# First 320 tokens of q and k by two other rings in float32, two pairs' scores in other banks, and the end by column halves

## The chip, the cores and the metric

The kernel runs on one core of one Trainium2 chip. The metric is device microseconds per execution, the median of several runs. Before: 324.33 us (three runs, 324.32 to 324.61). Executions of the kernel before fall into a fast state and a slow one, some 2% longer; only fast runs are compared. Ratios below are the mean time of one kernel's fast runs over the mean time of the other's fast runs of the same rounds, so they are not quite the ratio of the medians that stand beside them. The experiments ran on several chips, each beside runs of the kernel before on the same chip.

## The reference, cut to what matters

```python
B, H, S, D = 8, 8, 576, 64                      # batch, heads, tokens, head dim; all float32
scores = q @ k^T / sqrt(D), only |i - j| <= 32 kept
x = (softmax(scores) @ v)  -> (4608 tokens, 512)
h = x @ w_in                                    # 512 x 2048
g = where(h > 0, h, exp(min(h, 0)) - 1)
out = g @ w_out                                 # 2048 x 512
```

A banded attention feeds a feed-forward network (FFN). The FFN's matmuls are most of TensorE's work; the attention of the first pairs of query blocks has to be done before the FFN can start, while weights and later batches still load.

## The kernel before

Batch 0's q and k come by GpSimd's DMA queue, cast to bf16 on the way. Two heads share the 128 partitions (head `a` of a pair on partitions 64a to 64a+63, nine tokens in each partition):

```python
def load_qk(b, nm, half):
    src = {"q": q, "k": k}[nm]
    src = src[b, half * HP:(half + 1) * HP]          # four heads, all 576 tokens
    ...
    src = src.rearrange("(n a) (p t) d -> (a p) n (t d)", a=2, t=TPW)   # TPW = 9
    nc.gpsimd.dma_start(out=t, in_=src)
```

Scores, softmax, the transposed inputs of the FFN, and the end:

```python
def QK(i):
    psS = psS_p.tile([128, 2, 2, HP, QB], FP32, name="psS", tag="psS")   # one buffer
    ...
def SM(i):
    nc.scalar.activation(pu, live.pop(("S", i)), AX.Exp, scale=SCALE)
...
NPX = 8            # x of pairs 0 to 7 transposed by TensorE, of all later ones by DMA
...
def YC(t, c):      # last block: two copies of half the columns each, one after the other
    nc.scalar.copy(y[:, 0:DM // 2], ys[t, c][:, 0:DM // 2])
    nc.vector.tensor_copy(y[:, DM // 2:DM], ys.pop((t, c))[:, DM // 2:DM])
```

The instructions are ordered by a plan, a list of operations with ranks and dependences; `RING` is the order of GpSimd's loads (q, k, v and the quarters of w_in and w_out).

The softmax here doesn't subtract the row's maximum and nothing guards it: scores larger than these inputs give would overflow.

Of the kernel before, what the change touches and what calls it, by code (L numbers as in the profile page):

```python
# [156 lines left out]
def kernel(  # L157
# [20 lines left out]
    PR = 96  # L178
    TPP = S // PR
    TPW = S // QB  # L180
    NWB = 3
# [7 lines left out]
    const = ctx.enter_context(tc.tile_pool(name="const", bufs=1))  # L189
    bfp = ctx.enter_context(tc.tile_pool(name="bfp", bufs=4))  # L190
# [29 lines left out]

    def make_masks():
        mf = ep.tile([128, 4, QB], FP32, name="mf", tag="e")
        nc.gpsimd.memset(mf, 1.0)
        for mi in range(3):
            m = mf[:, mi, :]
            nc.gpsimd.affine_select(
                out=m, in_=m, compare_op=ALU.is_ge, fill=0.0,
                base=0, pattern=[[-1, QB]], channel_multiplier=1)
            nc.gpsimd.affine_select(
                out=m, in_=m, compare_op=ALU.is_ge, fill=0.0,  # L230
                base=2 * WIN, pattern=[[1, QB]], channel_multiplier=-1)
        for lo, key in ((0, QB), (QB, 0)):
            m = mf[lo:lo + QB, 3, :]
            nc.gpsimd.affine_select(
                out=m, in_=m, compare_op=ALU.is_ge, fill=0.0,
                base=key, pattern=[[-1, QB]], channel_multiplier=1)
            nc.gpsimd.affine_select(
                out=m, in_=m, compare_op=ALU.is_ge, fill=0.0,
                base=2 * WIN - key, pattern=[[1, QB]], channel_multiplier=-1)
        nc.gpsimd.affine_select(  # L240
            out=mf[:, 1, :], in_=mf[:, 1, :], compare_op=ALU.is_ge,
            fill=0.0, base=-WIN, pattern=[[0, QB]], channel_multiplier=1)
        nc.gpsimd.affine_select(
            out=mf[:, 2, :], in_=mf[:, 2, :], compare_op=ALU.is_ge,
            fill=0.0, base=(128 - WIN) - 1, pattern=[[0, QB]],
            channel_multiplier=-1)
        nc.gpsimd.tensor_copy(masks, mf)


    def wide(b):  # L250
        return b < NWB

    def load_qk(b, nm, half):
        src = {"q": q, "k": k}[nm]
        src = src[b, half * HP:(half + 1) * HP]
        if half == 0:
            live[nm, b] = bfp.tile(
                [128, HP, TPW * D] if wide(b) else [PR, H, TPP * D], BF16,
                name="bf", tag="bf")
        t = live[nm, b]  # L260
        if wide(b):
            t = t[:, half * HP // 2:(half + 1) * HP // 2]
            src = src.rearrange("(n a) (p t) d -> (a p) n (t d)", a=2, t=TPW)
        else:
            t = t[:, half * HP:(half + 1) * HP]
            src = src.rearrange("h (p t) d -> p h (t d)", t=TPP)
        nc.gpsimd.dma_start(out=t, in_=src)  # L267

    def T(b, nm, hp):
        src = live[nm, b]  # L270
        n = 2 * hp + (nm == "k")
        pool, tag = (psH_p, "psH") if b == 0 and n % 4 else (psT_p, "psT")
        pt = pool.tile([128, TPW, QB] if wide(b) else [128, TPP, PR], BF16,
                       name=tag, tag=tag)
        live["T", b, nm, hp] = pt
        if wide(b):
            for j in range(TPW):
                for a in (0, QB):
                    nc.tensor.transpose(pt[a:a + QB, j, :],  # L279
                                        src[a:a + QB, hp, j * D:(j + 1) * D],  # L280
                                        ident[a:a + QB, a:a + QB])
            return
        for j in range(TPP):
            nc.tensor.transpose(pt[:, j, :],
                                src[:, 2 * hp:2 * hp + 2, j * D:(j + 1) * D],
                                ident[0:PR, 0:PR])

    def E(b, nm, hp):
        pt = live.pop(("T", b, nm, hp))
        if nm == "k":  # L290
            dst = kT[b % NKB][:, hp, WIN:WIN + S]
        else:
            dst = qT[b % NKB][:, hp, :]
        dst = dst.rearrange("c (p t) -> c p t", t=TPW if wide(b) else TPP)
        src = pt.rearrange("c t p -> c p t")
        if EVAC[b, nm, hp] == "ACT":
            nc.scalar.copy(dst, src)  # L297
        else:
            nc.vector.tensor_copy(dst, src)  # L299
# [59 lines left out]
    def QK(i):  # L359
        psS = psS_p.tile([128, 2, 2, HP, QB], FP32, name="psS", tag="psS")  # L360
        for s in range(2):
            b, qb = divmod(2 * i + s, NQB)
            for h in range(H):
# [7 lines left out]
                for p0, p1, c in parts:  # L371
                    nc.tensor.matmul(  # L372
                        psS[p0:p1, h % 2, s, hp, :],
# [4 lines left out]
    def SM(i):  # L378
        pu = pup.tile([128, 2, 2, HP, QB], BF16, name="pu", tag="pu")
        nc.scalar.activation(pu, live.pop(("S", i)), AX.Exp, scale=SCALE)  # L380
# [32 lines left out]
    def RN(i, g):  # L413
        o = live.pop(("O", i, g))
        if g == 0:
            live["X", i] = xsp.tile([128, H, D], BF16, name="xs", tag="xs")
# [6 lines left out]
    def X(i):  # L423
# [6 lines left out]
        if i >= NPX:  # L430
# [52 lines left out]
    def ypool(t, c):  # L483
        if t < NT - 1:
            return psY_p, "psY"
        return ((psY_p, "psY"), (psO_p, "psO"), (psT_p, "psT"),
                (psS_p, "psS"))[c % 4]

    def Y(t, c, part):
        if part == 0:  # L490
            pool, nm = ypool(t, c)
            ys[t, c] = pool.tile([128, DM], FP32, name=nm, tag=nm)
        ps = ys[t, c]
        for fo in range(YQ * part, YQ * part + YQ):
            nc.tensor.matmul(ps, lhsT=gs[t][:, fo, c * 128:(c + 1) * 128],  # L495
                             rhs=w_out_sb[:, fo, :],
                             start=(fo == 0), stop=(fo == NFO - 1))

    def YC(t, c):
        y = yp.tile([128, DM], FP32, name="y", tag="y")  # L500
        if (t, c) == yseq[-1]:
            nc.scalar.copy(y[:, 0:DM // 2], ys[t, c][:, 0:DM // 2])
            nc.vector.tensor_copy(y[:, DM // 2:DM], ys.pop((t, c))[:, DM // 2:DM])
        else:
            nc.scalar.copy(y, ys.pop((t, c)))  # L505
        ys[t, c] = y

    def OUT(t, c):
        r = (tiles[t][0] + c) * 128
        y = ys.pop((t, c))  # L510
        if (t, c) == yseq[-1]:
            nc.sync.dma_start(out[r:r + 128, 0:DM // 2], y[:, 0:DM // 2])
            nc.scalar.dma_start(out[r:r + 128, DM // 2:DM], y[:, DM // 2:DM])
        else:
            nc.sync.dma_start(out[r:r + 128, :], y)
# [13 lines left out]
    NPX = 8  # L529

    P = Plan({"SP": 0.8, "ACT": 0.8, "POOL": 0.8, "DVE": 6.0})
# [20 lines left out]
    def prank(i):  # L552
# [3 lines left out]
    NV3 = 4  # L556
    LQ0, LQD = 64.0, 2.4
# [5 lines left out]
    RING = [  # L563
        ('L', 0, 'q', 0),
# [3 lines left out]
        ('ID',),  # L568
        ('LV', 0, 0),
        ('LV', 0, 2),  # L570
        ('MS',),
# [3 lines left out]
        ('WI', 1),  # L575
        ('L', 1, 'q', 0),
        ('L', 1, 'k', 0),
        ('WI', 2),
        ('LV', 0, 8),
        ('WI', 3),  # L580
        ('L', 1, 'q', 1),
        ('L', 1, 'k', 1),
        ('WO', 0),
        ('LV', 1, 0),
        ('WO', 1),
        ('LV', 1, 2),
        ('WO', 2),
        ('LV', 1, 4),
        ('WO', 3),
        ('L', 2, 'q', 0),  # L590
        ('L', 2, 'k', 0),
        ('LV', 1, 6),
# [19 lines left out]
    for b in range(B):  # L612
# [22 lines left out]
        for half in range(2) if b < XB else ():  # L635
            for nm in ("q", "k"):
                n = ("L", b, nm, half)
                deps = []
                if b >= 2:
                    deps += [("T", b - 2, nm, hp) for hp in range(HP)]  # L640
                P.op(n, "POOL", 0.75, RING.index(n) - 999, deps,
                     lambda b=b, nm=nm, half=half: load_qk(b, nm, half),
                     dma=1.5 if wide(b) else 1.7, wt=0.1, soft=ring(n))
# [4 lines left out]
        for qb in range(0, NQB, 2):  # L648
# [3 lines left out]
                 deps + (gate(x) if b >= XB else []),  # L652
# [19 lines left out]
        for hp in range(HP) if b < XB else ():  # L672
            for nm in ("q", "k"):
                n = hp * 2 + (nm == "k")
                deps = [("L", b, nm, hp // 2), ("ID",)]
                m = n - (4 if b == 0 else 1)
# [4 lines left out]
                P.op(("T", b, nm, hp), "PE", 0.5 if wide(b) else 0.3, need - 36 + 4 * n, deps,  # L681
                     lambda b=b, nm=nm, hp=hp: T(b, nm, hp))
                deps = [("T", b, nm, hp)]
# [5 lines left out]

    P.op(("ID",), "POOL", 0.6, RING.index(("ID",)) - 999, [],  # L690
# [10 lines left out]
    for i in range(NPAIR):  # L701
# [3 lines left out]
                for hp in range(HP) if b < XB]  # L705
# [7 lines left out]
        if i:  # L713
            deps.append(("SM", i - 1))
        P.op(("QK", i), "PE", 0.5, r, deps, lambda i=i: QK(i))
# [3 lines left out]
        P.op(("SM", i), "ACT", 1.05, r, deps, lambda i=i: SM(i))  # L719
        deps = [("SM", i), ("MS",)]  # L720
# [4 lines left out]
        for g in range(2):  # L725
            deps = [("MK", i)]
            for x in (2 * i, 2 * i + 1):
# [3 lines left out]
                else:  # L731
                    deps += [("SV", b, w0) + x for w0, w1 in SVOF[b]
                             if w0 <= qb < w1
                             for x in (((0,), (1,)) if b < 2 else ((),))]
            if i < NC0:
# [16 lines left out]
        if i < NPX:  # L752
            if i:
# [9 lines left out]
    for n, (t, fo) in enumerate(hseq):  # L763
# [4 lines left out]
        if n >= 3:  # L768
            deps.append(("GG",) + hseq[n - 3])
        if t >= 2:  # L770
# [16 lines left out]
    for n, (t, c) in enumerate(yseq):  # L787
        for part in range(NQ):
            r = (PER * (tiles[t][0] + tiles[t][1])
                 + 2 * YSP.get(t, 1) * (c * NQ + part) + 1)  # L790
            deps = [("GG", t, fo) for fo in range(YQ * part, YQ * part + YQ)]
            deps.append(("WO", part * YQ * NWC // NFO))
# [4 lines left out]
            elif c == 1:  # L797
                deps.append(("RN", NPAIR - 1, 1))
            P.op(("Y", t, c, part), "PE", 0.86, r, deps,
                 lambda t=t, c=c, part=part: Y(t, c, part))  # L800
        deps = [("Y", t, c, NQ - 1)]
# [7 lines left out]
    with tc.manual_schedule():  # L809
        for t in vw:  # L810
            nc.vector.memset(t[0:WIN, 0, :, 0:D], 0.0)
            nc.vector.memset(t[128 - WIN:128, NQB - 1, :, 0:D], 0.0)
            nc.vector.memset(t[:, 0:NQB:2, :, D:VW], 1.0)
        for t in kT:
            nc.vector.memset(t[:, :, 0:WIN], 0.0)
            nc.vector.memset(t[:, :, WIN + S:KW], 0.0)
        for t in pm:
            nc.vector.memset(t[:, :, QB:2 * QB], 0.0)
# [29 lines left out]
```

## Time and profile before

| what, profile of before | value |
|---|---|
| span (profiled run slow: 330.86 us, clock 0.993) | 329.0 us |
| TensorE busy | 306.6 us (93%) |
| first softmax, fourth softmax | 15.26, 21.00 us |
| first FFN matmul | 25.47 us |
| first output matmul, fourth output block | 38.53, 47.56 us |
| last store issued, end | 326.28, 329.0 us |

### The profile page before, as it was taken

How to read it: one execution, taken by the hardware profiler on the slowest of the kernel's cores; microseconds unless marked ns; L12 is line 12 of the kernel's file. 1: busy time of each engine (PE TensorE's matmuls, PEld its weight loads, DVE VectorE, ACT ScalarE, POOL GpSimd, SP SyncE). 2: the span in 40 equal slices, each digit the busy share in tenths (PEclk: the TensorE clock that was granted, in tenths of full speed). 3: DMA queues.
4: the chain of work that ended last, by engine and by line, in shares of the span. 5: the costliest groups of instructions: out<-in, count | busy, mean ns of one | idle time of the engine just before them, and what ended most of it. 6: DMA issues, size and time to landing. Idle time of an engine off the chain costs nothing.

```text
span 329.0 us, 7515 instructions
## 1 busy us (share of the span) xinstructions
PE 306.6 (93%) x2896; PEld 161.1 (49%) x2896; DVE 210.8 (64%) x500; ACT 196.6 (60%) x333; POOL 108.1 (33%) x203
## 2 busy tenths in 40 slices
PE   1579998899969999999999999999999999999995
PEld 1467765555524445444444444444445444444442
DVE  4584787668866777777666766666666666545500
ACT  2257987788735555555666666666666666555611
POOL 8934447935543544334546344100000000000000
PEclk9999999999997999999999999999999999999999
DMA  7999999999999999999999999933111112000021
GB/s 99 137 203 203 196 195 185 146 158 167 120 138 201 185 161 154 185 163 141 171 120 154 181 165 150 133 80 83 48 51 48 50 54 77 32 34 32 32 96 64
DMA packets 140371, 41.04 MB, mean 125 GB/s; under 512 B 125360, under 2 KB 135856, under 8 KB 140336
## 3 DMA queue, kind: packets, MB, share of 16 engines
q0 software_dynamic: 91872, 18.36, 74.6%
q1 hardware_dynamic: 48320, 22.08, 34.6%
q8 instruction: 22, 0.36, 0.5%
q10 hardware_dynamic: 144, 0.13, 0.1%
q14 instruction: 13, 0.11, 0.1%
HBM read 36.70 MB, written 9.44 MB: 140 GB/s over the span
## 4 chain that ended last, share of the span: by engine, by line
PE 84%; DMA 6%; POOL 4%; ACT 2%; DVE 2%; issue 1%; ACTq 0%; POOLq 0%
PE psH L452 37%; PE psY L495 34%; PE psO L405 5%; DMA bf<-in_q_dram 3%; PE psS L372 3%; DMA xt<-xs 3%; PE psT L279 2%; PE psS L495 1%; PE psO L495 1%; PE psT L495 1%; POOL vw L336 1%; POOL bf L267 1%; ACT e L460 1%; PE psT L435 1%; ACT kT L297 1%
## 5 line engine op out<-in xcount | busy, mean ns | idle before, releaser
L452 PE MATMUL psH<-xt,w_in_sb 128*128 128x512 bf16 (+1 forms) x640 | 150.9, 365 | 3.4 <-DMA xt<-xs 3.2
L460 ACT ACTIVATE e<-psH 128x512 f32<-128x512 f32 (+1 forms) x160 | 88.5, 554 | 93.2 <-PE psH L452 92.4
L495 PE MATMUL psY<-w_out_sb,g 128*128 128x512 bf16 x528 | 134.2, 379 | 0.0
L452 PEld LDWEIGHTS <-w_in_sb 128*128 128x128 bf16 x640 | 60.1, 100 | 60.7 <-DMA xt<-xs 3.7
L495 PEld LDWEIGHTS <-g 128*128 128x128 bf16 x576 | 52.6, 98 | 56.0
L478 DVE SCALAR_TENSOR_TENSOR g<-f,psH 128x512 bf16<-128x512 bf16 (+1 forms) x72 | 44.9, 624 | 34.6 <-ACT f L470 34.6
L472 DVE TENSOR_SCALAR f<-e 128x512 bf16<-128x512 f32 (+1 forms) x88 | 37.9, 430 | 38.6 <-ACT e L460 38.5
L481 DVE TENSOR_TENSOR g<-psH,f 128x512 bf16<-128x512 f32 (+1 forms) x88 | 56.5, 642 | 3.2
L470 ACT ACTIVATE f<-e 128x512 bf16<-128x512 f32 (+1 forms) x72 | 41.9, 582 | 2.2
L380 ACT ACTIVATE pu<-psS 128x1024 bf16<-128x1024 f32 x36 | 36.7, 1020 | 7.2 <-PE psS L372 6.2
L336 POOL DMA_DIRECT2D vw<-in_v_dram x40 | 33.7, 844 | 15.2 <-DMA w_in_sb<-in_moe_w_in_dram 3.4
L405 PEld LDWEIGHTS <-pm 128*128 128x128 bf16 x576 | 27.3, 101 | 14.3 <-issue 0.5
L308 POOL COPY scr<-g 1x1 bf16<-1x1 bf16 x73 | 14.8, 203 | 58.0 <-DVE g L481 48.3
L420 DVE TENSOR_TENSOR xs<-psO,rc 128x256 bf16<-128x256 f32 x68 | 28.8, 424 | 2.4
L405 PE MATMUL psO<-vw,pm 128*128 128x65 bf16 x544 | 28.7, 196 | 0.3 <-DVE xs L420 0.3
L393 DVE TENSOR_TENSOR pm<-pu,masks 128x512 bf16<-128x512 bf16 x72 | 27.0, 417 | 1.6 <-ACT pu L380 1.5
L317 POOL DMA_DIRECT2D bf<-in_k_dram x25 | 21.0, 840 | 7.6 <-issue 5.8
L317 POOL DMA_DIRECT2D bf<-in_q_dram x25 | 21.0, 840 | 5.3 <-issue 4.1
L505 ACT COPY y<-psY 128x512 f32<-128x512 f32 x33 | 18.8, 570 | 5.0 <-PE psY L495 5.0
L418 DVE RECIPROCAL rc<-psO 128x4 f32<-128x4 f32 x68 | 12.3, 181 | 14.6 <-PE psO L405 14.1
L372 PEld LDWEIGHTS <-kT 64*128 64x128 bf16 (+1 forms) x640 | 12.1, 102 | 14.9 <-issue 11.9
L372 PE MATMUL psS<-qT,kT 64*128 64x64 bf16 (+1 forms) x640 | 16.9, 199 | 2.5 <-DVE kT L299 1.3
(47 smaller groups left out, 98.4 us busy)
## 6 DMA issues: line engine op xcount, KB each, us to landing
out_dram<-y SPq DMA_DIRECT2D x35, 256.0 KB, 2.9
vw<-vw SPq DMA_DIRECT2D x12, 260.0 KB, 6.0
vw<-in_v_dram POOLq DMA_DIRECT2D x24, 128.0 KB, 5.8
bf<-in_k_dram POOLq DMA_DIRECT2D x20, 128.0 KB, 5.7
bf<-in_q_dram POOLq DMA_DIRECT2D x20, 128.0 KB, 5.6
w_in_sb<-in_moe_w_in_dram POOLq DMA_DIRECT2D x4, 512.0 KB, 12.4
w_out_sb<-in_moe_w_out_dram POOLq DMA_DIRECT2D x4, 512.0 KB, 13.8
bf<-in_q_dram POOLq DMA_DIRECT2D x6, 288.0 KB, 10.9
```

Of the source, the lines that this page charges most:

```text
L317: nc.gpsimd.dma_start(out=live["N", nm, b][0:n, j, :].rearrange("p (h d) -> p h d", d=D), in_=src[128 * j:128 * j + n])
L336: nc.gpsimd.dma_start(out=vt[r:r + hi - lo, qb, :, 0:D], in_=vb[lo:hi])
L372: nc.tensor.matmul(psS[p0:p1, h % 2, s, hp, :], lhsT=kT[b % NKB][base:base + 64, hp, c:c + p1 - p0], rhs=rhs, start=True, stop=True)
L380: nc.scalar.activation(pu, live.pop(("S", i)), AX.Exp, scale=SCALE)
L405: nc.tensor.matmul(o[:, j, :], lhsT=p[:, h, s * QB:s * QB + 128], rhs=vw[b % NVB][:, qb, h, :], start=(s == 0), stop=(s == 1))
L452: nc.tensor.matmul(ps, lhsT=w_in_sb[:, do, fo * 128:(fo + 1) * 128], rhs=xts[t][:, do, :], start=(do == 0), stop=(do == NDO - 1))
L460: nc.scalar.activation(e, ps, AX.Exp)
L470: nc.scalar.activation(f, e, AX.Relu, bias=1.0, scale=-1.0)
L472: nc.vector.tensor_scalar(f, e, -1.0, 0.0, ALU.add, ALU.min)
L478: nc.vector.scalar_tensor_tensor(gs[t][:, fo, :], f, -1.0, ps, ALU.mult, ALU.max)
L481: nc.vector.tensor_tensor(gs[t][:, fo, :], ps, f, ALU.max)
L495: nc.tensor.matmul(ps, lhsT=gs[t][:, fo, c * 128:(c + 1) * 128], rhs=w_out_sb[:, fo, :], start=(fo == 0), stop=(fo == NFO - 1))
```

## The change

The intent: start attention earlier by bringing the first 320 tokens of q and k of batch 0 on the two hardware rings (SP's and ACT's), in float32 and with casts on VectorE and ScalarE, while GpSimd makes masks; let the scores of pairs 1 and 3 use two FFN banks so that they need not wait for the softmax before them; transpose x of pair 11 on TensorE; and end by column halves so that the last two copies are not in a row. The core of the diff:

```diff
+    TPA = 5
...
+    def load_first(nm, hp):
+        src = {"q": q, "k": k}[nm][0, 2 * hp:2 * hp + 2, 0:QB * TPA]
+        (nc.scalar if nm == "q" else nc.sync).dma_start(
+            out=live["F", nm][:, hp],
+            in_=src.rearrange("a (p t) d -> a p (t d)", t=TPA))
+    def cast_first(nm, h):
...
+        if nm == "k":
+            nc.scalar.copy(dst, src)
+        else:
+            nc.vector.tensor_copy(dst, src)
...
     def load_qk(b, nm, part):
+        if b == 0:                       # the other 256 tokens, one pair of heads per load
+            hp, c0, c1 = part, TPA, TPW
+            nc.gpsimd.dma_start(
+                out=dst[:, hp, c0 * D:c1 * D],
+                in_=src[2 * hp:2 * hp + 2, QB * c0:QB * c1].rearrange(
+                    "a (p t) d -> a p (t d)", t=c1 - c0))
...
     def QK(i):
+        if i in ALT:                     # ALT = (1, 3)
+            psS = [psH_p.tile([128, 2, HP, QB], FP32, name="psH", tag="psH")
+                   for _ in range(2)]
...
-    NPX = 8
+    NPX = (*range(8), 11)
...
+    CL1, CLD = -900, [("E", 0, "k", 0)]  # second buffers' memsets: after the first k eviction
...
     def Y(t, c, part):                   # last block: 256 columns at a time, in two banks
...
+    def YCL(h):
+        nc.scalar.copy(y, ys.pop((t, c, h)))
+        for n, eng in enumerate((nc.sync, nc.scalar)):
+            eng.dma_start(out[r + 64 * n:r + 64 * n + 64, cols],
+                          y[64 * n:64 * n + 64])
```

RING also changes: identity and masks first, then eight small loads between v loads, and two v loads of batch 1 move behind w_out's last quarter.

## The prediction

> **What bounds the kernel now.** I read the page first. TensorE is busy for 306.6 of 329.0 us, so the question is where the other 22 us lie and where a busy TensorE is not at its pace.
>
> ```profile
> PE   1579998899969999999999999999999999999995
> PEclk9999999999997999999999999999999999999999
> DMA  7999999999999999999999999933111112000021
> GB/s 99 137 203 203 196 195 185 146 158 167 120 138 201 185 161 154 185 163 141 171 120 154 181 165 150 133 80 83 48 51 48 50 54 77 32 34 32 32 96 64
> ```
>
> A slice is 8.2 us. TensorE is short of work in the first two or three slices and a little at the end; the DMA engines are at 9 from the second slice on, and move some 200 GB/s (counted in bf16 bytes, since these loads cast; the float32 read is twice that).
>
> Second, the timeline of the start. First transposes 5.30, first score matmuls 12.77, first softmax 15.26, first FFN matmul 25.47. Third, the waits of TensorE in order of time, the chain, and GpSimd's waits, which tell when loads land, because it has eight in flight and waits for the one eight back:
>
> ```profile
> 5.30 0.69 PE L279 MATMUL psT<-ident,bf 64*64 64x64 bf16 x18 [5.30 <-DMA bf<-in_q_dram]
> 15.26 1.02 ACT L380 ACTIVATE pu<-psS 128x1024 bf16<-128x1024 f32 x1 [3.68 <-PE psS L372]
> 16.33 0.76 PE L372 MATMUL psS<-qT,kT 64*128 64x64 bf16 x24 [1.12 <-ACT pu L380]
> 20.06 0.70 POOL L267 DMA_DIRECT2D bf<-in_k_dram  x1 [2.02 <-DMA w_in_sb<-in_moe_w_in_dram]
> 24.85 0.69 PE L279 MATMUL psT<-ident,bf 64*64 64x64 bf16 x18 [1.17 <-DMA bf<-in_q_dram]
> ...
> 40.87 0.78 POOL L336 DMA_DIRECT2D vw<-in_v_dram  x1 [1.22 <-DMA w_out_sb<-in_moe_w_out_dram]
> 44.24 0.70 POOL L267 DMA_DIRECT2D bf<-in_k_dram  x1 [1.08 <-DMA w_out_sb<-in_moe_w_out_dram]
> 47.65 0.88 POOL L336 DMA_DIRECT2D vw<-in_v_dram  x1 [1.28 <-DMA w_out_sb<-in_moe_w_out_dram]
> ```
>
> So w_in's first quarter lands at 20.0, and w_out's second, third and fourth quarters at 40.8, 44.2 and 47.6. The output matmuls that need these three start at 41.21, 44.75 and 47.56. That is the important reading: until 48 us the PE's order is paced by the weight stream, not by attention. No wait of TensorE names it, because its order was fitted to arrivals.
>
> Fourth, the end:
>
> ```profile
> 325.42 0.37 ACT L502 COPY y<-psS 128x256 f32<-128x256 f32 x1 [2.87 <-PE psS L495]
> 325.82 0.42 DVE L503 COPY y<-psS 128x256 f32<-128x256 f32 x1 [13.15 <-ACT y L502]
> 326.28 0.37 ACTq L513 DMA_DIRECT2D out_dram<-y  x1
> ```
>
> The two last copies are in a row, 0.40 us apart, and the last store needs 329.0 - 326.28 = 2.7 us.
>
> Fifth, one stall in the middle, which this profile shows and the timed runs may not:
>
> ```profile
> 98.63 1.48 PE L452 MATMUL psH<-xt,w_in_sb 128*128 128x512 bf16 x4 [3.18 <-DMA xt<-xs]
> ```
>
> The profiled run took 330.86 us against 324.33 timed and counts as slow. After the stall the clock digit is 7; stall plus throttled matmuls (0.37 us each instead of 0.216) make about 5 of those 6.5 us. Most timed runs can't have all of it.
>
> **Pure matmul work.** From the chain: four 128x512 take 0.86, eight 128x256 0.87, 18 load transposes 0.40, 24 score matmuls 0.47, eight AV 0.24, four xs transposes 0.22. Over the whole program: H 124.4, Y 124.4, AV 17.3, scores 12.5, transposes 9.6 + 1.8 = 290 us. "Lag" below is time minus the pure work issued before that point. In the kernel before it is 18 at the first FFN matmul, 21.8 at the first output matmul (38.53), 22.65 at the fourth output block (47.56, after 24.9 us of work), and 27.4 at 88 us: the growth after 48 is the single psT bank, whose transposes and copies on ScalarE take turns (2.5 us of "PE psT <- ACT kT"). From 104 us on a pair of blocks takes 7.84 us against 7.86 of work: nothing to win there.
>
> **What the Trainium skill says.**
> - "DMA: Bandwidth & Descriptors", Issuing engines are not separate DMA queues: loads from SP, ACT and GpSimd share the same 16 engines and several issuers save only issue time. Before's DMA row of nines agrees that the engines, not issue, are full from 8 us on. So the new rings can bring data sooner only where the engines idle.
> - The same page, Anatomy of one DMA: about 2 us fixed. The first load here lands 5.29 - 2.15 = 3.1 us after its issue ended; last store 2.35 after.
> - "ScalarE: Activation LUTs", What ACT_TABLE_LOAD costs: about 1283 ns. The trace has 1.28, at 0.81 us, where it costs nothing.
> - "TensorE: Matmul & The Clock Gate", What's actually happening: idle gates the clock to half. The stall above agrees.
>
> **The change, part by part.**
>
> 1. First 320 tokens by two hardware rings. Eight loads of 164 KB, float32, 1.31 MB; at the 400 GB/s source rate of the later loads that is 3.3 us, so from about 1.7 to 5.5 us (estimate). Casts: 128x640, 0.5 us on DVE, 0.7 on ACT (from 0.43 and 0.55 for 512 elements). In the instruction order the table load now stands behind ACT's four issues and carries one of the casts' DMA waits, so 1.28 us falls after the k load: ACT casts near 5.5. 2.9 us of memsets now stand on DVE between the two k evictions, so I put the second k eviction at 10.7 to 11.5, the first scores near 11.5 and the first softmax near 12.5: 2.8 us earlier.
>
> 2. Scores of pairs 1 and 3 in the FFN banks: the second score block no longer waits 1.12 us for the softmax; two exps of 512 cost 0.2 more than one of 1024. Softmaxes came every 1.9 us; they become nearly adjacent, except for evictions. The fourth goes from 21.0 to about 16.5. Together 1 and 2 gain some 4 us in attention.
>
> 3. What it does to the load stream. GpSimd now makes identity and masks first (0.6 + 4.0 us, from 1.2 to 5.8), then issues eight small loads of about 0.6 and four v loads of 0.87, so the first w_in quarter is issued near 14.6 instead of 12.9. The engines finish the hardware loads at 5.5, idle until about 7.5, and are issue-fed from there; v moves at only about 95 GB/s (bf16; 11 to 15 us of before), so the v loads end near 16.4. Before, they ended near 15.0. All bytes up to w_out's first quarter are the same. So the weight stream comes 1.4 us LATER: w_out's first quarter about 39.2 instead of 37.8.
>
> 4. The reordered ring gives some back: two v loads of 128 KB move from before w_out's last quarter to behind it (2 x 0.65 us). That quarter then lands at 47.6 + 1.4 - 1.3 = 47.7, but TensorE's new order has 26.0 us of work before the block that needs it instead of 24.9. Lag there: 21.7 instead of 22.65. Gain 0.9 us. This is the term that I believe in, not the 4 us of attention: the rest waits for weights.
>
> 5. xs of pair 11 by TensorE: adds 0.22 us of PE and one 0.59 us copy. Removes the 98.63 stall where it exists: 0 to 3.2 us, and up to 1.7 of throttle with it. I count 1.2 net.
>
> 6. The end by column halves: same work (two 128x256 for one 128x512, 0.108 each), first half stored 1.7 us earlier, last copy 0.37 and then two stores at once. Takes off the 0.40 of the serial copies, and 0.06 of issue: 0.45.
>
> Sum: 0.9 + 1.2 + 0.45 = 2.5 us; 324.33 - 2.5 = 321.8.
>
> **Rivals.**
> - A: attention is the bound and all of its 4 us arrive. For it: TensorE is idle 11.6 of the first 24 us. Against: the arrivals that coincide with the output matmuls. Then 4 + 1.6 = 5.6, 318.7 us.
> - B: the weights come even later (GpSimd's small loads cost 0.72 like the large ones, or v is issue-bound): another 1 to 2 us, nothing left of step 4, about 323.5 to 324.5.
> - C: timed runs have the whole stall of pair 11 and its throttle: 5 us instead of 1.2, giving 318.
> - D: the psT chain from 48 to 66 us absorbs any start gain, since its order is about as tight as before: 322.7.
>
> **Range and chances.** A and C alone stop just short of 2% (317.84); both together, or one with a lucky order, pass it: 0.11. A loss over 2% needs a new stall of 6.5 us, which nothing shows: 0.01. Predicted 321.8, range 318.4 to 324.0.
>
> **What would show it.** Right: first softmax near 12.5 and fourth near 16.5; w_in's first quarter landing after 20.5; TensorE waiting for weights between 24 and 40 us where it waited for nothing; the output blocks starting within 0.5 us of before's times, the fourth near 47.7 with 1.1 us more done; no xt wait near 98; last copy to end 0.45 shorter. Wrong: the first output matmul at 36 or earlier (A), a DMA stream that is ahead of before at 16 us, or a gain that appears after 50 us.

## More of the kernel before

The queue that GpSimd feeds, as packets, MB and share of the time of 16 engines, and the issues of q by that queue with their size and their time to landing:

```profile
q0 software_dynamic: 91872, 18.36, 74.6%
bf<-in_q_dram POOLq DMA_DIRECT2D x6, 288.0 KB, 10.9
```

All of q and k goes through this one queue. (The size is counted in bf16; the read is twice that.)

## The result, and the profile after

The changed kernel is slower: 352.08 us (351.12 to 352.91, four runs) against 324.47 for the kernel before in the same rounds; ratio 1.084, 95% interval 1.0794 to 1.0887. The result is correct, the profiled run is fast, its span 351.2 us and its clock 1.000. The predicted 321.8 us, and the range up to 324.0, were wrong by 28 us.

TensorE's busy time hardly changed (305.3 us); the 40 slices, 8.8 us each now, show where the time went:

```profile
PE   0010688998899999999999999999999999999995
DMA  2932999999959999999999999984221121010022
GB/s 33 96 58 49 157 202 204 198 169 163 172 98 160 169 172 141 187 196 176 138 174 142 153 169 167 147 128 82 73 66 45 48 60 47 30 62 30 30 75 76
```

The first four slices of TensorE are all but empty. So is the DMA row in slices 1, 3 and 4 (digits 2, 3 and 2, with 58 and 49 GB/s), while the kernel before ran it at 9 from its second slice on. A long pause in which the DMA engines are also idle is not a lack of bandwidth: something holds the transfers. The wait list of TensorE names the casts (columns: what waited, for whom, us in total, times, longest):

```profile
PE psT L321 <- DVE bf L282: 22.4, 1, 22.4
PE psH L321 <- DVE bf L282: 11.4, 1, 11.4
PE psS L413 <- DVE kT L334: 2.3, 1, 2.3
```

And the timeline of the start (start, duration, engine, line, operation; in brackets the idle time before it and what ended it) says what the casts waited for:

```profile
0.81 13.64 SPq L269 DMA_DIRECT2D stg<-in_k_dram  x4
0.81 17.38 ACTq L269 DMA_DIRECT2D stg<-in_q_dram  x4
18.28 1.28 ACT L280 ACT_TABLE_LOAD   x1 [18.28 <-DMA stg<-in_k_dram]
20.63 0.92 POOL L371 DMA_DIRECT2D vw<-in_v_dram  x1 [8.96 <-DMA bf<-in_q_dram]
21.83 0.49 DVE L282 CAST bf<-stg 128x640 bf16<-128x640 f32 x1 [19.06 <-DMA stg<-in_q_dram]
32.77 0.72 ACT L280 CAST bf<-stg 128x640 bf16<-128x640 f32 x1 [8.91 <-DMA stg<-in_k_dram]
34.44 0.57 DVE L282 CAST bf<-stg 128x640 bf16<-128x640 f32 x1 [12.11 <-DMA stg<-in_q_dram]
40.43 1.02 ACT L426 ACTIVATE pu<-psS 128x1024 bf16<-128x1024 f32 x1 [2.98 <-PE psS L413]
```

The first half of q is on hand at 21.8 us and the last at 34.4; the prediction had all eight loads landed by 5.5. Even the four issues took ScalarE's queue 17.38 us. GpSimd's own small loads suffer too (8.96 us of waiting at 20.63), so w_in's first quarter is issued at 35.80 us instead of 12.14. How much moved meanwhile stands in a window in which hardly anything but the first loads moved (the last three columns: clock, share of the 16 DMA engines' time, GB/s):

```profile
24.00:26.00 2.00, 0.00 (x0) 0.00 (x0) 0.00 (x0) 0.00 (x0) 0.00 (x0) 1.00 0.14 46
```

0.14 of 16 engines is 2.2 engines, and 46 GB/s is 23 GB/s for each of two. At 46 GB/s the eight loads of 164 KB (1.31 MB) need 28 us.

Two engines is also what the built program lets one expect. In `load_first` only 320 of a head's 576 tokens are read, so head and partition no longer merge: the source is `[[36864,2],[320,64],[1,320]]`, with a dimension of **2** outermost. The Trainium skill, page "DMA: Bandwidth & Descriptors", section "Why a DMA increments its semaphore by 16 and not by 1", says how many engines a DMA takes: the largest number up to 16 that divides the slowest dimension (of a size other than 1) of both access patterns; and that a load of GpSimd's queue can be an exception and take 16. The destination's 128 and the source's 2 leave 2. The trace agrees with its 0.14; it does not list the engines one by one. Its packets agree too. These are the packets of one of the two rings up to 45 us, first in the changed kernel, then in the run below in which the first loads alone are cut otherwise:

```profile
q10 hardware_dynamic: 520, 0.66, 3.9%
```

```profile
q10 hardware_dynamic: 576, 0.66, 6.1%
```

The four loads of a ring have 4 x 128 rows, so 512 packets in both. What is left is 8 packets here and 64 there, 2 and 16 for each load: the counts that one closing packet from each engine would give.

| profile | before (slow run) | after |
|---|---|---|
| span | 329.0 us | 351.2 us |
| first softmax | 15.26 | 40.43 |
| first FFN matmul | 25.47 | 50.72 |
| first output matmul | 38.53 | 67.99 |
| TensorE busy | 306.6 | 305.3 |

### The profile page after: what moved, and what is told of

It is laid out like the page before. It is cut to its first block, busy times and chain, and to the rows that moved or that the text cites. A ratio compares the mean times of both kernels' runs of the same rounds, so it can differ in the third digit from the quotient of the medians.

```text
span 351.2 us, 7582 instructions
## 1 busy us (share of the span) xinstructions
PE 305.3 (87%) x2916; PEld 162.5 (46%) x2916; DVE 210.6 (60%) x501; ACT 198.8 (57%) x339; POOL 111.7 (32%) x207
## 3 DMA queue, kind: packets, MB, share of 16 engines
q0 software_dynamic: 99104, 17.73, 72.9%
## 4 chain that ended last, share of the span: by engine, by line
PE 83%; DMA 7%; DVE 3%; ACT 3%; ACTq 2%; issue 1%; DVEq 0%
PE psH L498 36%; PE psY L549 33%; DMA stg<-in_q_dram 7%; PE psO L451 5%; PE psS L413 3%; ACTq L269 2%; PE psO L549 1%; PE psT L321 1%; PE psT L549 1%; ACT e L506 1%; PE psT L481 1%; DVE pm L439 1%; ACT qT L332 1%; PE psS L549 1%; DVE kT L334 0%
## 5 line engine op out<-in xcount | busy, mean ns | idle before, releaser
L549 PEld LDWEIGHTS <-g 128*128 128x128 bf16 x592 | 54.2, 98 | 54.6
L426 ACT ACTIVATE pu<-psS 128x1024 bf16<-128x1024 f32 x34 | 34.7, 1020 | 5.4 <-PE psS L413 5.3
L321 PE MATMUL psT<-ident,bf 64*64 64x64 bf16 x324 | 9.5, 207 | 23.3 <-DVE bf L282 22.4
L321 PEld LDWEIGHTS <-bf 64*64 64x64 bf16 x432 | 10.7, 128 | 39.8 <-DVE bf L282 33.9
```

Source lines behind the costliest of these rows:

```text
L426: nc.scalar.activation(pu, live.pop(("SS", i)), AX.Exp, scale=SCALE)
L549: nc.tensor.matmul(ps, lhsT=gs[t][:, fo, c * 128:(c + 1) * 128], rhs=w_out_sb[:, fo, cols], start=(fo == 0), stop=(fo == NFO - 1))
```

## The experiments

**The theory**: the two-head dimension outermost puts each of the eight first loads on two DMA engines, and this alone is the loss. **Rivals**: the small loads of GpSimd's queue, which have the same cut, are held in the same way and matter as much; the two hardware rings or float32 rows are slow as such; the FFN banks or the new order cost it. Twelve kernels ran. All gave correct results.

### Both parts of the load recut, one at a time and together

The recut puts one head of each of two pairs into a load, 64 partitions wide, so that the partitions (64) come outermost: source `[[320,64],[73728,2],[1,320]]`. Bytes, number of DMAs, rings and row length stay the same.

```diff
 def load_first(nm, hp):
-    src = {...}[nm][0, 2 * hp:2 * hp + 2, 0:QB * TPA]
+    h, a = divmod(hp, 2)
+    src = {...}[nm][0].rearrange("(n a) s d -> a n s d", a=2)
+    src = src[a, 2 * h:2 * h + 2, 0:QB * TPA]
     (nc.scalar if nm == "q" else nc.sync).dma_start(
-        out=live["F", nm][:, hp],
-        in_=src.rearrange("a (p t) d -> a p (t d)", t=TPA))
+        out=live["F", nm][64 * a:64 * a + 64, 2 * h:2 * h + 2],
+        in_=src.rearrange("n (p t) d -> p n (t d)", t=TPA))
```

The second recut is the same for the small loads in `load_qk` (tokens 320 to 575).

Only the first loads recut:

> The eight float32 loads of the first 320 tokens alone are cut differently: one head of each of two pairs (64 partitions x 2 x 320) instead of the two heads of one pair (source outermost dimension 2). Same bytes, same number of DMAs, same rings. Fan-out theory (the old cut ran on 2 of 16 engines, some 24 GB/s each): they land by 7 us instead of 34, first scores near 12 instead of 37, but the eight small GpSimd loads, still cut the old way, hold the second part of q and k until about 28 us; total 335 to 345. Rival, the rings themselves are slow (1280-byte rows, descriptors made by SP and ACT): the loads still land near 34 us, total 350 to 353. Rival, the GpSimd loads are the whole trouble: no change, 350 to 353.

Measured 329.32 us (two runs), ratio 1.0128 (1.0076 to 1.018), span 327.4: nearly the whole loss is gone with one edit of one access pattern, and up to 291 GB/s move between 3 and 6 us:

```profile
3.00:4.00 1.00, 0.00 (x0) 0.00 (x0) 0.00 (x0) 0.00 (x0) 0.88 (x4) 1.00 1.18 270
...
5.00:6.00 1.00, 0.00 (x0) 0.00 (x0) 0.00 (x0) 0.00 (x0) 1.00 (x2) 1.00 0.93 291
```

(Packets of several queues overlap, so that the share of the engines' time can pass 1.) The time is below the expected range: the small loads landed 6.5 to 7.4 us after their issue (shown below) and did not hold the second part of q and k until 28 us, as I had thought they might.

Only the small loads recut:

> The eight small GpSimd loads (tokens 320 to 575 of batch 0) alone are cut differently, the float32 loads as in the changed kernel. Fan-out theory: the float32 loads share their two engines with nothing and land near 28 us instead of 34; first scores near 31, total 343 to 349. Ring theory: 350 to 353. GpSimd-load theory: first scores near 12, total 320 to 326.

Measured 355.65 us (two runs), ratio 1.0937 (1.0881 to 1.0993): not faster than the changed kernel, and rather slower (the changed kernel's interval, 1.0794 to 1.0887, just touches this one). The expectation missed. What the trace shows: the small loads go off faster, GpSimd comes to the first quarter of w_in at 21.51 instead of 35.80, and its traffic now runs beside the first loads, which still have the old cut; the last k cast falls back from 32.77 to 35.19. The one probably causes the other; no run shows it alone. The two lines:

```profile
21.51 0.81 POOL L597 DMA_DIRECT2D w_in_sb<-in_moe_w_in_dram  x1 [4.89 <-DMA vw<-in_v_dram]
35.19 0.72 ACT L280 CAST bf<-stg 128x640 bf16<-128x640 f32 x1 [11.64 <-DMA stg<-in_k_dram]
```

Both recut:

> Both sets cut differently; all else is the changed kernel. Fan-out theory: all of the loss goes, and what is left is what I forecast for the change, 321.8 (319 to 324), with the first softmax near 12.5, the fourth near 16.5, w_in's first quarter landing after 20.5 and the fourth output block near 47.7. Ring theory: still over 345.

Measured 328.01 us (four runs), ratio 1.0074 (1.0027 to 1.0121), span 326.2. The start, to be held against the timeline of the changed kernel:

```profile
0.81 2.99 SPq L271 DMA_DIRECT2D stg<-in_k_dram  x4
0.82 2.71 ACTq L271 DMA_DIRECT2D stg<-in_q_dram  x4
6.02 0.49 DVE L284 CAST bf<-stg 128x640 bf16<-128x640 f32 x1 [3.25 <-DMA stg<-in_q_dram]
6.66 1.28 ACT L282 ACT_TABLE_LOAD   x1 [6.66 <-DMA stg<-in_k_dram]
8.45 0.49 DVE L284 CAST bf<-stg 128x640 bf16<-128x640 f32 x1 [1.94 <-DMA stg<-in_q_dram]
13.50 0.76 DVE L338 COPY kT<-psH 128x640 bf16<-128x640 bf16 x1
15.02 1.02 ACT L430 ACTIVATE pu<-psS 128x1024 bf16<-128x1024 f32 x1 [3.22 <-PE psS L417]
```

The issues take 3.0 and 2.7 us instead of 13.6 and 17.4, and the first half of q is on hand at 6.0 instead of 21.8. Same rings, same float32 rows, same bytes: the rival that blames the rings or the data type for the 28 us falls, and so do the banks and the order, which were not touched. The theory holds for 7.1 of the 8.4% by the first loads alone. (The total missed the expected 319 to 324, and the first softmax is hardly earlier than before; that comes below.)

The small loads' share, as issues up to 45 us, first of the run with the old cut of the small loads, then with the new one (last column: us to landing):

```profile
bf<-in_q_dram POOLq DMA_DIRECT2D x4, 64.0 KB, 6.5
bf<-in_k_dram POOLq DMA_DIRECT2D x4, 64.0 KB, 7.4
```

```profile
bf<-in_q_dram POOLq DMA_DIRECT2D x4, 64.0 KB, 3.4
bf<-in_k_dram POOLq DMA_DIRECT2D x4, 64.0 KB, 3.1
```

And that queue's packets over the whole program, first of the changed kernel, then with both recut:

```profile
q0 software_dynamic: 99104, 17.73, 72.9%
```

```profile
q0 software_dynamic: 91936, 17.70, 76.7%
```

With the old cut these eight loads make 7,168 more packets and land twice as late. The extra packets carry next to nothing: 17.73 - 17.70 = 0.03 MB, some 4 bytes each. So on GpSimd's queue the same cut shows in another way than on the rings. It costs about 0.5% (1.0128 against 1.0074; the intervals overlap, but both runs with the old cut, 329.10 and 329.53, lie above all four with the new one, 326.33 to 328.32, on the same chip).

### The end by column halves alone, on the kernel before

```diff
 # in the kernel before: ypool, Y, YCL and the last block's dependences as in the change
-    nc.scalar.copy(y[:, 0:DM // 2], ys[t, c][:, 0:DM // 2]) ...
+    def YCL(h): ...
```

> The kernel before with the end by column halves alone. My forecast for this part was 0.45 us off (323.9). Rival, from the changed kernel's trace, where the span ends 3.67 us after the last group of matmuls starts to be evicted, as against 3.65 before: nothing, 324.2 to 324.6.

Measured 325.0 us (six runs, one of them slow), ratio 0.9995 (0.9965 to 1.0025): nothing that the timed runs resolve, to which the forecast 0.45 us would be 0.0014. The trace of the end has to tell:

```profile
319.60 0.37 ACT L521 COPY e<-psS 128x256 f32<-128x256 f32 x1 [1.37 <-PE psS L503]
320.00 0.50 ACTq L524 DMA_DIRECT2D out_dram<-e  x1
```

The serial copy of 0.40 is gone, but the end comes 323.3 - 319.97 = 3.3 us after the last copy's end, where the kernel before took 329.0 - 326.24 = 2.8. The stores of 64 rows were issued in 0.50 (0.37 with 128 rows), and the rest is a later landing: 323.3 - 320.50 = 2.8 us, against 329.0 - 326.65 = 2.35. (The profile of before was a slow run. The pair-11 run below is a fast one with the old end, and gives 322.4 - 319.53 = 2.9 after the last copy and 322.4 - 319.94 = 2.5 for the landing.) The saving is given back. SP's two stores stand as one row there, the second issued at about the same time as ACT's; which of the two lands last the trace does not say.

This trace is worth more as a **fast** profile of the kernel before, whose order of instructions on each engine is the same up to the last block, at 315.9 us. In it the fourth softmax is at 20.60, the fourth output block at 46.81, and no stall stands near 98 us:

```profile
20.60 1.02 ACT L380 ACTIVATE pu<-psS 128x1024 bf16<-128x1024 f32 x1 [0.16 <-PE psS L372]
46.81 1.02 PE L503 MATMUL psY<-w_out_sb,g 128*128 128x512 bf16 x3 [0.41 <-DMA w_out_sb<-in_moe_w_out_dram]
```

Here TensorE does wait 0.41 us for w_out's last quarter: for the fourth block the reading that weights pace it is confirmed. The three blocks before it name no such wait in this trace.

### Pair 11 by TensorE alone, on the kernel before

```diff
-    NPX = 8
+    NPX = (*range(8), 11)
```

> The kernel before with one part of the change alone: pair 11's inputs are transposed by TensorE instead of by the DMA. The prediction's step 5 put this at 1.2 us net saved (a stall of 1.6 us in the profile of before, less 0.4 us of extra matmul work), so about 323.3 us against 324.5. The rival: the profile of before fell in its slow state (329.0 us of span), and the fast trace of the tail experiment shows no such stall, so the timed fast runs have nothing to save there and the extra work of some 0.3 us is lost or hidden: 324.3 to 325.0 us, a ratio of 1.000 to 1.001. Below 323.7 speaks for the step, above 324.2 for the rival.

Measured 324.74 us (six runs, all fast), ratio 0.9992 (0.9963 to 1.0022). The profiled run was 1.12 us ahead of the end-by-halves run before pair 11 and 0.90 ahead after it (times of the same ScalarE exps of the FFN): by these two traces the part costs 0.2 us and saves nothing, since a fast run has no stall there. The timed runs alone could not tell: their interval reaches from 1.2 us of gain to 0.7 of loss. The rival fits both.

### The memsets first

With both loads recut the first softmax was still at 15.0, because the second k eviction (13.50 above) stands behind 3.1 us of memsets for the second buffers (from 10.38). They are moved to VectorE's idle time before the first cast. The plan then chose another order in which a transpose could have read a half-written block, so the transposes also got a second dependence.

```diff
-    CL1, CLD = -900, [("E", 0, "k", 0)]
+    CL1, CLD = -998, []
...
-        deps = [("RN", i, 1)]
+        deps = [("RN", i, 0), ("RN", i, 1)]
```

> On top of the version with both loads cut differently (328.0 us): the 2.9 us of memsets of the second buffers go to DVE's idle time before the first cast instead of between two evictions of k. (The transposes of xs now name both halves of xs as what they wait for: the other order of the plan needs it.) Theory that the attention chain at the start is the loss: first softmax near 12.3 instead of 15.0, first FFN matmul near 24 instead of 26, total 325.5 to 327. Theory that weights pace everything until 48 us: no change, 327.5 to 328.5. Theory that TensorE's half pace until 33 us is the loss: little, unless the matmuls reach full pace earlier; 326.5 to 328.5.

Measured 325.89 us (four runs), ratio 1.0023 (0.9991 to 1.0055), as the theory of the attention chain at the start had it (325.5 to 327) and not that of the weights (327.5 to 328.5); but the plan's order changed with it, so the memsets alone are not shown to be what helped. Softmaxes, a GpSimd issue that waited for w_out's last quarter, and the fourth output block:

```profile
13.27 1.02 ACT L430 ACTIVATE pu<-psS 128x1024 bf16<-128x1024 f32 x1 [1.36 <-PE psS L417]
14.79 1.09 ACT L428 ACTIVATE pu<-psH 128x512 bf16<-128x512 f32 x2
19.36 1.02 ACT L430 ACTIVATE pu<-psS 128x1024 bf16<-128x1024 f32 x1 [3.00 <-PE psS L417]
20.58 1.09 ACT L428 ACTIVATE pu<-psH 128x512 bf16<-128x512 f32 x2 [0.20 <-PE psH L417]
...
47.42 1.03 PE L553 MATMUL psY<-w_out_sb,g 128*128 128x512 bf16 x4
47.64 0.69 POOL L302 DMA_DIRECT2D bf<-in_k_dram  x1 [1.82 <-DMA w_out_sb<-in_moe_w_out_dram]
```

The first two pairs come earlier, but the third and the fourth do not: 20.58 against 20.60 in the fast profile of before. The weight stream is where the prediction put it (last quarter at 47.6, foreseen 47.7), and the fourth block starts 0.61 us later than in the fast profile of before (46.81). The plan's new order has less work ahead of this block than the changed kernel's: against the kernel before, only four more matmuls of 128x256 (92 weight loads of w_in instead of 88, all others equal), so 25.35 instead of 24.91 us, and not the 26.04 of the prediction. The version with both loads recut and the order untouched does have the 26.04, and there its weights are early and the block late: GpSimd is released by w_out's last quarter at 47.41, and the block starts at 51.57:

```profile
47.41 0.69 POOL L302 DMA_DIRECT2D bf<-in_k_dram  x1 [1.82 <-DMA w_out_sb<-in_moe_w_out_dram]
51.57 1.03 PE L553 MATMUL psY<-w_out_sb,g 128*128 128x512 bf16 x4
```

So in that version weights did not pace the fourth block.

### v earlier

```diff
 RING: ('ID',), ('LV', 0, 0), ('LV', 0, 2), ('MS',), eight small loads, ...   # two v loads ahead of masks
```

> As the run before it, and the first two v loads go ahead of the masks and of the small q and k loads on GpSimd, as in the kernel before. If the first AV waits for v (it does in the trace of the version with both loads cut differently: 0.7 us for the v copy, 0.8 for the masked scores), the first AV starts near 14 instead of 17.3 and the total falls to 323.5 to 326. If only the order of the FFN part matters, as the run before it within 0.5 us.

Measured 326.76 us, ratio 1.0043 (1.0009 to 1.0077). A miss: the v copies come earlier, but the second half of k lands later (11.1 us), and the first product with v then waits for the k eviction instead.

### Without the FFN banks

```diff
-    ALT = (1, 3)
+    ALT = ()
```

on the version with both loads recut.

> The version with both loads cut differently, with the scores of pairs 1 and 3 back in the one score bank pair. If the FFN banks for scores are worth what I forecast (the second softmax right behind the first), this is 0.5 to 1.5 us slower than 328.0. If they are a cost (they hold three FFN banks and order TensorE badly), it is 0.5 to 1.5 us faster. If the start is paced by something else: 327.5 to 328.5.

Measured 329.08 us, ratio 1.0126 (1.0088 to 1.0164), against 1.0074 with the banks (on another chip; the intervals overlap). The fourth softmax is at 22.41 instead of 20.95. The banks are worth 1 to 2 us here, where attention is late; the change of dependences also changes the plan's order, so this is the worth of both.

### What the pauses of TensorE cost

With both loads recut and the memsets late, TensorE ran at half pace until 33 us. Here every transpose of batch 1's first q and k is done twice, 3.2 us of work that nobody needs:

```diff
-                for a in (0, QB):
+                for a in (0, QB) * (1 + (b == 1)):
```

> The version with both loads cut differently, with each of the 144 load transposes of batch 1 done twice (same result, 3.2 us more matmul work at full pace), to keep TensorE busy between 25 and 40 us. Clock theory (TensorE runs at half pace until 33 us because it has gaps, and that is 2.8 us of the loss): full pace (four 128x256 in 0.60) by 29 us, total 327 to 329. Rival (the half pace is no cause): full pace no earlier, total 331 to 333.

Measured 328.33 us, ratio 1.0098 (1.0067 to 1.0129). First a row of the version without the extra work, then one with it:

```profile
29.74 1.06 PE L502 MATMUL psH<-xt,w_in_sb 128*128 128x256 bf16 x4
```

```profile
30.63 0.60 PE L502 MATMUL psH<-xt,w_in_sb 128*128 128x256 bf16 x4
```

The same four matmuls take 1.06 us in one and 0.60 in the other: with useless work in the pauses TensorE is at full pace earlier (30.6 instead of 33.1; one profile each), and the ratio rises by 0.0024, some 0.8 us, for 3.2 us of added work (the two ran on different chips, and the intervals overlap). So up to 2.4 us of the added work cost nothing (3.2 - 0.8, an estimate). How much of this is the earlier full pace, and how much is work that merely filled idle time and would have been free at any pace, the run does not separate. What half pace at the start cost is therefore not shown. The section that the prediction cited ("TensorE: Matmul & The Clock Gate", "What's actually happening") says that idle gates the clock to half; the four matmuls agree. The row of granted clock, PEclk, does not show it: it reads 9 in every slice of both runs.

### The table load early, the same with doubled transposes, and the memsets again

A copy of one column on ScalarE right after its load issues takes the table load out of the path:

```diff
+        if nm == "q" and hp == HP - 1:
+            nc.gpsimd.memset(early, 0.0)
+            nc.scalar.copy(early[:, 1:2], early[:, 0:1])
```

> The version with both load cuts mended and the second buffers' memsets moved to the front, and besides a copy of one column on ScalarE right after it issued its loads, so that its table load (1.28 us, at 7.24 us in the run without it, between the landing of the first k and its cast) falls into the wait for the loads. If the table load paces the start, the first k cast moves from 8.5 to about 7.3 us and the first softmax from 13.3 to about 12.1. If the weights then pace the first four output blocks as in that run (last quarter at 47.6 us), the total hardly moves: 325.3 to 325.9 us. If the start still counts, 324.5 to 325.2. Rival: VectorE is nearly full between 10 and 24 us and takes the gain; then the first softmax is early but the first FFN matmul stays near 24.7 us and the total near 325.9.

Measured 327.03 us (six runs), ratio 1.0062 (1.0028 to 1.0096). The table load moved to 3.54 us and the first softmax from 13.27 to 12.51, but the first FFN matmul stayed (24.84 against 24.69): the second rival in the expectation. Then TensorE was at half pace until about 31 us. The next two runs ask whether that explains why it is not better:

> The version with the early table load, and besides every transpose of batch 1's first q and k done twice: some 3.2 us of extra TensorE work in the first 30 us, the result unchanged. That version started its first softmax at 12.5 us but ran TensorE at half pace until about 31 us (8 matmuls of 128x256 in 1.89 us at 28.45) where the version without the early table load was at full pace from 26, and its first output matmul came at 41.0 us instead of 39.1. If the pauses of TensorE between 14 and 25 us, which keep the clock at half pace, cost those 2 us, the doubled work fills pauses, full pace comes by 27 to 28 us, and the total falls by 0.5 to 1.5 us to 325.5 to 326.5. If TensorE's work itself or VectorE sets that stretch, the total rises by up to 3 us, to 327.5 to 330.

> The version with both load cuts mended and the second buffers' memsets first, run again beside the previous one so that the two are compared on the same chip: it gave 1.0023 of the kernel before on another chip, and the version with the early table load 1.0062 here. If the early table load really loses time through the clock, this stays at 1.000 to 1.004 (324.5 to 326.3 us); if the difference was between chips, 1.005 to 1.008.

The rows of the FFN matmuls at 28 us, first with the early table load, then with doubled transposes besides:

```profile
28.45 1.89 PE L506 MATMUL psH<-xt,w_in_sb 128*128 128x256 bf16 x8
```

```profile
28.30 1.05 PE L506 MATMUL psH<-xt,w_in_sb 128*128 128x256 bf16 x8
```

Full pace came three us earlier, as foreseen, but the total was 326.92 us, ratio 1.008 (1.0049 to 1.0111): about the same time with 3.2 us more work, and not the gain that I had expected. That the doubling brought the earlier pace is not certain either: the memsets-first version, without any filler, took 1.05 us for the same eight matmuls at 27.90 in its run here. It gave 326.45 us on this third chip, ratio 1.0049 (1.0028 to 1.007), between my two expectations. So the early table load is no gain, and whether it is a small loss stays open (1.0062 and 1.0049 have overlapping intervals). None of the twelve kernels beats the kernel before; the two parts alone equal it, the memsets-first version is 0.2 to 0.5% behind it.

Where that remainder sits shows in the same ScalarE exps of the memsets-first run and the fast profile of before. About level at 95.5 us (95.52 against 95.56; the exps around it lie up to 1.6 us off, since the orders differ), 0.46 us behind from 116 to 140 us, 0.98 from 164 us to the end. The second step is one wait, for a transposed x by DMA:

```profile
154.90 1.02 PE L502 MATMUL psH<-xt,w_in_sb 128*128 128x512 bf16 x4 [0.36 <-DMA xt<-xs]
```

It is a stall of the kind that the slow profile of before has at 98.63, in another place. What makes the first 0.46 I did not settle; 0.2 of it may be pair 11's extra work.

## Why the prediction was wrong

**Step 1, the term that failed**: "Eight loads of 164 KB, float32, 1.31 MB; at the 400 GB/s source rate of the later loads that is 3.3 us, so from about 1.7 to 5.5 us". The runs show 46 GB/s and the last landing at 34.4 us. I took a rate from transfers with 128 partitions outermost and gave it to transfers with 2 outermost, without looking at the access patterns. With the recut (same rings and bytes) the cast of the first half of q starts at 6.0 us and that of the last half at 8.45, after a wait for its load. So even for a load that uses all the engines the estimate was some 3 us short, but not 29. That this term is the loss is proved by the recut alone: ratio 1.084 to 1.0128, some 23 us of the 27.6.

The rest of that step foresaw the table load behind a k DMA and the memsets between the k evictions, but not their sum: with both recut the first softmax came at 15.0, not 12.5; with memsets moved at 13.3; with the table load moved too at 12.5.

**Step 2** was wrong in its size: "The fourth goes from 21.0 to about 16.5". In the memsets-first version it came at 20.58. ScalarE waits 3.00 us there for the third pair's scores, which TensorE begins only at 18.50, behind the first product with v; this one waited 1.56 us for a copy of v on VectorE (until 17.59), which stood behind the k evictions of the second part. The banks help by 1 to 2 us when attention is late.

**Step 3** held in its direction once the loads were mended. In the memsets-first version GpSimd is released by w_in's first quarter at 22.23 us (21.50 in its run on the other chip), against 19.46 in the fast profile of before: 2.0 to 2.8 us later, not 1.4. W_out's last quarter came at 47.6, as foreseen, which is 0.6 later than in that fast profile (47.05).

**Step 4** ("Gain 0.9 us") failed in two ways. It was measured against the profile of a slow run: there the lag at the fourth block was 22.65; in the fast profile it is 46.81 - 24.91 = 21.9. The version with the predicted order reached 51.57 - 26.04 = 25.5 (foreseen 21.7). So its block did not start with its weights, as the step has it, but 4.2 us after them. The memsets-first version reached 47.42 - 25.35 = 22.1. At that point there was no gain in either.

**Step 5** ("I count 1.2 net") was, by the traces, a loss of 0.2: the stall was one of the slow profile. The prediction said so ("which this profile shows and the timed runs may not") and still counted it for 1.2.

**Step 6** ("0.45") was 0 in the trace: later landing of the 64-row stores gave the saving back.

So even without the fault in step 1 the sum of 2.5 us was not there: none of its three terms was reached. Of the **rivals**, B is nearest to the mended kernel; none contained what happened. The sentence "A loss over 2% needs a new stall of 6.5 us, which nothing shows: 0.01" was the overconfident one: the diff showed it, in a slice that keeps 320 of 576 tokens, so that two dimensions can no longer merge.

## What to carry to other kernels

When a load's slice or rearrangement changes, write down both access patterns and look at the outermost count before giving the load any rate; a head count of 2 in front of the partitions held the load at 46 GB/s where up to 291 were to be had, and regrouping the heads so that the partitions came outermost cured it. When a small term rests on one stall, look whether the profiled run was as fast as the timed ones. In a start-up phase, look at the third and fourth pair and at TensorE's pace, not only at the first softmax.

## What the Trainium skill lacked or had wrong

- The rule that decided this was not lacking: "DMA: Bandwidth & Descriptors" has it in the section on semaphores and again among its rules for kernel authors, and the prediction used that page without it. What the page has no number for is the cost: eight hardware-ring loads with 2 outermost moved 46 GB/s and landed up to 34.4 us; with 64 outermost all eight were on hand by 9.2 us.
- The same page lists some 27 GiB/s (29 GB/s) per engine under "Specifications". Two engines moved 46 GB/s here, 23 GB/s each, with rows of 1,280 bytes.
- The same page doesn't say that such loads also block the engine that issues them: four issues took ScalarE's queue 17.38 us, against 2.71 with the recut.
- The page's exception for GpSimd's queue fits (no fall to two engines was seen), but no page that I read says that the same cut makes more packets there: 7,168 more, of some 4 bytes, for eight loads of 64 KB, which landed after 6.5 to 7.4 us instead of 3.1 to 3.4.
- On no page I read: stores of 64 rows by 256 columns in two halves were issued in 0.50 instead of 0.37 us and ended 2.8 instead of 2.35 to 2.5 us after the issue, which ate the 0.40 us saved.
